# Attention in groups of four heads and channel mix in 384-token units: one change to a fused kernel on one Trainium2 core

## The chip, the core and the metric

The kernel runs on one core of one Trainium2 chip. The metric is the device time of one execution in microseconds (us); every kernel tried was run four times, alternating with the kernel before on the same chip. The engines are TensorE (PE in the profile, PEld for its weight loads), VectorE (DVE), ScalarE (ACT), GpSimd (POOL) and the DMA engines, fed from queues on SyncE (SP), ScalarE and GpSimd. Each of VectorE, ScalarE and GpSimd works through its own instruction list in the order that the compiled program gives it.

## The reference, cut to what matters

```python
# q, k, v: (8 batches, 8 heads, 576 tokens, 64) fp32
q_s = softmax(q, axis=-1)                 # over the 64 channels of a token
k_s = softmax(k, axis=2)                  # over the 576 tokens
kv  = einsum('bhsd,bhse->bhde', k_s, v)   # 64 x 64 per head
x   = einsum('bhsd,bhde->bhse', q_s, kv)  # then heads side by side: (8, 576, 512)

x_prev = x shifted by one token
xk = mu_k * x + (1 - mu_k) * x_prev       # the same with mu_r for xr
k  = relu(xk @ w_k)                       # 512 x 1024
v  = (k * k) @ w_v                        # 1024 x 512
out = sigmoid(xr @ w_r) * v               # w_r 512 x 512
```

## The kernel before

The kernel works batch by batch. Attention handles two heads at a time (a "pair", 4 per batch): the two heads lie on the two halves of the partitions, and products have 64 weight columns. v is loaded by GpSimd's queue, which casts fp32 to bf16 on the way, two loads per pair. The parts that the change touches:

```python
def emit_attention_pair(b, hp):
    nc.gpsimd.dma_start(out=va[0:64, :, 0:64],    in_=v_src_A)    # casting loads
    nc.gpsimd.dma_start(out=va[64:128, :, 65:129], in_=v_src_B)
    nc.scalar.activation(out=eqk, in_=QKt[:, hp, :, :], func=ACT.Exp)
    # ... VectorE: sum, reciprocal, qs = eq / sum
    for j in range(J):                                            # J = 9
        nc.tensor.matmul(kvp[:], lhsT=eqk[:, 1, j, :], rhs=va[:, j, :], ...)   # 64 columns
    # ... two ScalarE copies scale kv into kvpad; 9 transposes; two copies into qtpad
    nc.tensor.matmul(otp[0:64, 0:512],   lhsT=kvApad, rhs=qTApad[:, 0:512], ...)
    # ... three more: head A and B, columns 0:512 and 512:576
    nc.scalar.copy(out=xb[:, 64:64 + S], in_=otp[:])
    # ... VectorE: four scalings by mu or 1-mu, three additions (the last 64 tokens apart)

for b in range(B):                        # channel mix of batch b, attention of b + 1
    for fc in range(FT):                  # 8 steps: first matmuls, 288 tokens at a time
        emit_t3(b, fc); maybe_pairs(slot)   # the 4 pairs fall in these 8 steps
    for m in range(4):                    # 4 steps: output matmuls, 128 tokens at a time
        emit_t45(b, m)
    # ... 64 tokens per batch are left over and handled for two batches together
```

The softmax here doesn't subtract the row's maximum and nothing guards it: scores larger than these inputs give would overflow.

## Time and profile before

| what | value |
|---|---|
| time, median | 279.24 us at first, 279.57 with one more run |
| TensorE busy | 228.8 us, 83% |
| VectorE busy | 194.7 us, 70% |
| a steady batch | 28.4 us, and 2.6 us more in every second one |

These lines of the page of the profile before are the busy time by engine, the span in 40 slices (a digit is the busy share in tenths; PEclk is TensorE's granted clock), GpSimd's DMA queue, and the chain of waits by engine and by line.

```profile
PE 228.8 (83%) x1648; PEld 133.5 (48%) x1648; DVE 194.7 (70%) x636; ACT 154.4 (56%) x357; POOL 50.3 (18%) x73
PE   0045423999999899979997999989989999999992
DVE  5199804999689935997499828994899659755421
DMA  7999999993599447992599258944663352033044
q0 software_dynamic: 39984, 7.34, 36.6%
PE 56%; DVE 21%; DMA 12%; ACT 6%; issue 2%; POOL 1%
```

TensorE is nearly full from the eighth slice on (48 us), while VectorE swings between 9 and 3. The casting loads (of v, and once of the weights) make 39,984 packets and take 36.6% of the DMA engines' time for 7.3 MB.

TensorE stops at 36.6 us and starts again at 45.5, when a load of v that was queued behind the weights lands.

The windows view of before gives busy time per engine in the two halves of one steady batch: first matmuls with attention, then output matmuls. In both kernels its columns are start and end, length, then busy us (and instructions) of PE, PEld, DVE, ACT, POOL, then clock, DMA share and GB/s. (The DMA share counts the whole time of every packet that starts in the stretch, so it can exceed 1.)

```profile
105.70:123.20 17.50, 15.75 (x149) 10.61 (x147) 15.44 (x56) 15.17 (x37) 5.99 (x8) 1.00 1.22 195
123.20:134.10 10.90, 10.90 (x54) 4.89 (x54) 7.46 (x21) 3.50 (x9) 0.00 (x0) 1.00 0.44 57
```

In the first half TensorE and VectorE are both near 90%, each waiting for the other; in the second TensorE is full and VectorE, even with what it carried over, is not.

Durations overlap on VectorE, so costs are best read from start to start. Three lines of the timeline show it: each scaling is listed with 0.36 us, but the next starts 0.28 us later.

```profile
119.86 0.36 DVE L218 TENSOR_SCALAR xmk<-xb_111,muk 128x576 bf16<-128x576 bf16 x1
120.14 0.36 DVE L228 TENSOR_SCALAR xmr<-xb_111,mur 128x576 bf16<-128x576 bf16 x1
120.42 0.36 DVE L222 TENSOR_SCALAR xpk<-xb_111,omk 128x576 bf16<-128x576 bf16 x1
```

### The profile page before, as it was taken

The page shows a single profiled execution, that of the slowest core. Times are in us where ns is not written, and L with a number is a line of the kernel's source. Part 1 is how long each engine was busy: PE and PEld are TensorE (multiplying, and loading weights), DVE is VectorE, ACT ScalarE, POOL GpSimd, SP SyncE. Part 2 cuts the span into 40 slices and gives each one's busy share as a digit, 9 for nine tenths or more (in the row PEclk, how much of TensorE's full clock was granted, in tenths as well). Part 3 has the DMA queues.
Part 4 walks back from the last instruction along what each step waited for, and adds up shares of the span by engine and source line. Part 5 has one row for each costly group of instructions (what it writes and reads, how often), then busy time and mean ns, then how long its engine had stood idle before and what let it go on. Part 6 is the DMA issues. An engine that isn't in the chain of part 4 may idle for free.

```text
span 277.1 us, 4740 instructions
## 1 busy us (share of the span) xinstructions
PE 228.8 (83%) x1648; PEld 133.5 (48%) x1648; DVE 194.7 (70%) x636; ACT 154.4 (56%) x357; POOL 50.3 (18%) x73
## 2 busy tenths in 40 slices
PE   0045423999999899979997999989989999999992
PEld 0034302664466345644564446634654456546540
DVE  5199804999689935997499828994899659755421
ACT  2438403696398626892689239862887167626420
POOL 6027202230033102330224004210322020000000
PEclk9998555699999999999999999999999999999998
DMA  7999999993599447992599258944663352033044
GB/s 248 221 277 241 260 230 77 310 97 21 114 207 234 26 100 113 241 168 43 106 236 194 42 112 198 243 28 97 80 43 24 76 107 31 2 75 77 0 106 85
DMA packets 55368, 35.97 MB, mean 130 GB/s; under 512 B 40496, under 2 KB 42032, under 8 KB 55344
## 3 DMA queue, kind: packets, MB, share of 16 engines
q0 software_dynamic: 39984, 7.34, 36.6%
q1 hardware_dynamic: 10560, 18.88, 27.4%
q10 hardware_dynamic: 4800, 9.44, 11.4%
q8 instruction: 13, 0.21, 0.3%
q14 instruction: 11, 0.09, 0.1%
HBM read 33.56 MB, written 9.44 MB: 155 GB/s over the span
## 4 chain that ended last, share of the span: by engine, by line
PE 56%; DVE 21%; DMA 12%; ACT 6%; issue 2%; POOL 1%
PE vp L275 20%; PE kfpt L252 12%; PE rp L280 10%; DMA vaug_108<-in_v_dram 8%; PE kvp L179 3%; DMA mur<-in_moe_mu_r_dram 3%; PE vpt L299 2%; PE otp L205 2%; PE qtp L194 2%; DVE xk_b L225 2%; DVE xmr L228 2%; DVE rsum L169 2%; DVE qs L173 2%; DVE xr_b L235 2%; DVE xpr L232 2%
## 5 line engine op out<-in xcount | busy, mean ns | idle before, releaser
L252 PE MATMUL kfpt<-xk_b,wk_bf 128*128 128x288 bf16 x512 | 77.9, 293 | 4.2 <-DMA wk_bf<-in_moe_w_k_dram 3.6
L252 PEld LDWEIGHTS <-wk_bf 128*128 128x128 bf16 x512 | 46.1, 99 | 25.9 <-issue 6.4
L256 ACT ACTIVATE rel<-kfpt 128x288 bf16<-128x288 f32 x128 | 48.0, 408 | 8.0 <-PE kfpt L252 6.1
L284 ACT ACTIVATE th<-rp 128x512 f32<-128x512 f32 x32 | 19.1, 597 | 57.5 <-PE rp L280 57.4
L287 DVE SCALAR_TENSOR_TENSOR ot<-th,vp 128x512 f32<-128x512 f32 x32 | 22.0, 687 | 36.0 <-ACT th L284 36.0
L194 PE MATMUL qtp<-ident,qs 128*64 128x128 bf16 x288 | 25.3, 235 | 25.2 <-DVE qs L173 17.0
L163 ACT ACTIVATE eqk<-QKt 128x1152 bf16<-128x1152 f32 x32 | 37.2, 1168 | 1.7 <-PE kvp L179 1.4
L280 PE MATMUL rp<-wr_bf,xr_b 128*128 128x512 bf16 x128 | 33.4, 379 | 0.0
L194 PEld LDWEIGHTS <-qs 128*64 128x64 bf16 x288 | 20.2, 120 | 22.7 <-DVE qs L173 17.0
L179 PEld LDWEIGHTS <-eqk 128*64 128x64 bf16 x288 | 20.1, 119 | 19.3 <-issue 17.7
L169 DVE TENSOR_REDUCE rsum<-eqk 128x9 f32<-128x576 bf16 x32 | 23.3, 730 | 4.2 <-ACT eqk L163 4.2
L173 DVE TENSOR_TENSOR qs<-eqk,rrec 128x576 bf16<-128x576 bf16 x32 | 24.0, 753 | 0.6
L280 PEld LDWEIGHTS <-xr_b 128*128 128x128 bf16 x128 | 12.5, 98 | 15.3 <-issue 0.5
L159 POOL DMA_DIRECT2D vaug_108<-in_v_dram x11 | 8.0, 732 | 60.2 <-PE kvp L179 57.8
L159 POOL DMA_DIRECT2D vaug_104<-in_v_dram x11 | 8.3, 759 | 54.3 <-PE kvp L179 50.6
L214 ACT CAST xb_103<-otp 128x576 bf16<-128x576 f32 x11 | 7.0, 638 | 19.2 <-PE otp L211 19.2
L179 PE MATMUL kvp<-vaug_108,eqk 128*64 128x130 bf16 x99 | 9.6, 240 | 8.9 <-DMA vaug_108<-in_v_dram 8.9
L159 POOL DMA_DIRECT2D vaug_112<-in_v_dram x10 | 7.7, 769 | 46.0 <-PE kvp L179 46.0
L225 DVE TENSOR_TENSOR xk_b<-xmk,xpk 128x576 bf16<-128x576 bf16 x32 | 14.3, 447 | 0.0
L235 DVE TENSOR_TENSOR xr_b<-xmr,xpr 128x512 bf16<-128x512 bf16 x32 | 13.3, 415 | 0.0
L199 ACT COPY qtpad_105<-qtp 64x576 bf16<-64x576 bf16 x11 | 6.9, 628 | 8.4 <-PE qtp L194 8.4
L179 PE MATMUL kvp<-vaug_104,eqk 128*64 128x130 bf16 x99 | 9.9, 240 | 0.0
(227 smaller groups left out, 387.8 us busy)
## 6 DMA issues: line engine op xcount, KB each, us to landing
out_dram<-ot SPq DMA_DIRECT2D x64, 128.0 KB, 2.4
QKt<-in_q_dram SPq DMA_DIRECT2D x7, 1152.0 KB, 8.4
QKt<-in_k_dram ACTq DMA_DIRECT2D x7, 1152.0 KB, 10.5
vaug_104<-in_v_dram POOLq DMA_DIRECT2D x22, 72.0 KB, 6.2
vaug_108<-in_v_dram POOLq DMA_DIRECT2D x22, 72.0 KB, 6.3
vaug_112<-in_v_dram POOLq DMA_DIRECT2D x20, 72.0 KB, 6.4
QKt<-in_q_dram SPq DMA_DIRECT2D x4, 288.0 KB, 5.5
QKt<-in_k_dram ACTq DMA_DIRECT2D x4, 288.0 KB, 5.8
```

The costliest lines, as they stand in the source:

```text
L159: nc.gpsimd.dma_start(out=va[0:64, :, 0:64], in_=v_src_A)
L163: nc.scalar.activation(out=eqk[:].rearrange("p a j d -> p (a j d)"), in_=QKt[:, hp, :, :].rearrange("p a f -> p (a f)"), func=ACT.Exp)
L169: nc.vector.reduce_sum(out=rsum[:], in_=eq, axis=AX.X)
L173: nc.vector.tensor_tensor(out=qs[:], in0=eq, in1=rrec[:, :, None].to_broadcast((128, J, D)), op=ALU.mult)
L179: nc.tensor.matmul(kvp[:], lhsT=eqk[:, 1, j, :], rhs=va[:, j, :], start=(j == 0), stop=(j == J - 1))
L194: nc.tensor.transpose(out=qtp[:, 128 * j:128 * j + 128], in_=qs[:, j, :], identity=ident[:])
L225: nc.vector.tensor_tensor(out=xk_b[:, hp, :], in0=xmk[:], in1=xpk[:], op=ALU.add)
L252: nc.tensor.matmul(kfp, lhsT=wk_bf[:, ct, fc * 128:(fc + 1) * 128], rhs=xk_b[:, ct, c0:c1], start=(ct == 0), stop=(ct == CT - 1))
L256: nc.scalar.activation(out=rel[:, 0:(c1 - c0)], in_=kfp, func=ACT.Relu)
L275: nc.tensor.matmul(vp[0:M, 0:C], lhsT=k2[:, ft, t0:t0 + M], rhs=wv_bf[:, ft, :], start=(ft == 0), stop=(ft == FT - 1))
L280: nc.tensor.matmul(rp[0:M, 0:C], lhsT=xr_b[:, ct, t0:t0 + M], rhs=wr_bf[:, ct, :], start=(ct == 0), stop=(ct == CT - 1))
L287: nc.vector.scalar_tensor_tensor(out=ot[0:M, :], in0=th[0:M, :], scalar=1.0, in1=vp[0:M, 0:C], op0=ALU.add, op1=ALU.mult)
```

## The change

Its intent: make attention's matmuls use the whole array, make fewer and larger instructions everywhere, load v by plain fp32 loads, and spread attention evenly over the channel mix. Four heads form a group (2 per batch). The four 64x64 kv matrices of a group become two 128x128 block-diagonal weights w. The channel mix runs in units of 384 tokens over pairs of batches (1152 tokens, 3 units), so no 64-token rest remains. A unit has 14 steps (8 of first matmuls, 6 of output matmuls), and attention's steps are handed out over all of them.

```diff
-        nc.gpsimd.dma_start(out=va[0:64, :, 0:64], in_=v_src_A)
-        nc.gpsimd.dma_start(out=va[64:128, :, 65:129], in_=v_src_B)
+        for i, src in enumerate((q, k, v)):            # plain fp32, 4 heads each
+            nc.sync.dma_start(out=t[:, i, :, :], in_=ap)
+        nc.gpsimd.tensor_copy(out=vv[:, :, 0:128]..., in_=t[:, 2, :, :]...)   # cast
 ...
-            nc.tensor.matmul(kvp[:], lhsT=eqk[:, 1, j, :], rhs=va[:, j, :], ...)
+            for hf in range(2):
+                r = slice(64 * hf, 64 * hf + 64)
+                nc.tensor.matmul(kvp[:, hf, 0:129], lhsT=eqk[r, 1, j, :, :]..., rhs=vv[r, j, 0:129], ...)
+        for hf in range(2):                            # block-diagonal by a mask
+            nc.vector.scalar_tensor_tensor(out=w[:, hf, :], in0=kvp[:, hf, 0:128],
+                                           scalar=rz[:, hf:hf + 1], in1=mask[:], ...)
 ...
-        nc.tensor.matmul(otp[0:64, 0:512], lhsT=kvApad, rhs=qTApad[:, 0:512], ...)   # and 3 more
+                nc.tensor.matmul(xp[:, a, 0:288], lhsT=w[:, hf, :], rhs=qt[:, hf, 288 * a:288 * a + 288], ...)
 ...
-        for (c0, c1) in [(0, 288), (288, S)]:
+    def unit(n):                                       # 384 tokens
+        for fc in range(FT):
+            # 4 matmuls of 384 columns, one Relu, one square; yield
+        for m in range(U // 128):
+            # tanh part; yield; value part and output; yield
 ...
-    nc.gpsimd.dma_start(out=wv_st[:], in_=wv_src)
-    nc.vector.tensor_scalar(out=wv_bf[:], in0=wv_st[:], scalar1=0.5, ...)
+        for h in range(2):                             # after the casts of batch 0
+            nc.gpsimd.dma_start(out=wv_h, in_=ap)
+            nc.vector.tensor_scalar(out=wv_h, in0=wv_h, scalar1=0.5, ...)
 ...
+    for n in range(NU):                                # 12 units
+        goal = min((B - 1) * ASTEPS, ASTEPS + int(ASTEPS * n / 1.5) + 1)
+        for i, _ in enumerate(unit(n)):
+            want = goal0 + (goal - goal0) * (i + 1) // MSTEPS
+            # take attention steps until `want`
```

## The prediction

> **What bounds the kernel now.** TensorE, in three unequal stages. (1) Start: the timeline shows TensorE idle from 36.6 us to 45.5 us behind one v load (`vaug_108`), which the chain of waits carries as 21.3 us of DMA: it was queued behind the weights. Until then DMA moves 220 to 280 GB/s. (2) Seven steady batches of 28.4 us, plus 2.6 us for a tail in every second. The back-to-back starts in the timeline give, per batch, about 8.0 us of first matmuls, 10.4 us of output matmuls and 4 x 1.5 us of attention, 24.4 in all; some 4 us are stalls. They fall in the attention half, where VectorE is busy without a gap for 20 us, while in the output half VectorE idles (36.0 us waiting for tanh). (3) Last batch and tails, 27 us, pure TensorE at 0.97 clock.
>
> **What the change does to each engine.**
> - Channel mix on TensorE: same work. 384 matmuls of 384 columns instead of 512 of 288, and 432 of 512 as before. Estimate from starts 125 ns (288 columns) and 216 ns (512): 13 us per unit, 156 us in all.
> - Attention on TensorE: per four heads 18 kv matmuls on 64 rows, 9 transposes, 4 products of 288 columns: estimate 1.7 to 2.2 us at 62 ns a small one, against 3.06 us for two pairs. Saves 14 to 21 us over sixteen groups.
> - VectorE: one 1152-element pass replaces two of 576, two k2 squares of 288+224+64 become one of 384, no tail pieces. Net of overlap (start to start: scale 0.28, add 0.36, reduce 0.66, output 0.60 us) I estimate 7.7 us per group, 0.27 per square, 0.6 per output: about 21.4 us per batch against 22.8. But w moves here from ScalarE.
> - ScalarE: 6.6 us of attention per two pairs falls to 3.6. It was not the limit.
> - GpSimd: 64 casting loads (36.6% of DMA time in tiny packets, the queue table) vanish; 16 casts of v appear. The Trainium skill, "SBUF — State Buffer", section "Who interferes with whom", says that GpSimd and the two-port VectorE instructions lock each other out. The trace of before has no such cast; I allow 1 to 2 us per group.
>
> **Critical path.** Attention is now spread over all steps of a unit, so VectorE's load is even. In an attention unit (1.5 groups): TensorE 13 + 3.3 = 16.3 us, VectorE about 15.7 plus locks; with stalls 17 to 18. About 8.5 such units, then three of 13 us.
>
> **Start.** Batches 0 and 1 (7.1 MB) and weights (5.2 MB) must arrive before attention of batch 1 ends; at 250 to 270 GB/s that is 46 to 49 us, so the start gains little; but more is done by then.
>
> Sum: 49 + 8.5 x 17.5 + 3 x 13 + 3 = 240 us.
>
> **Predicted: 240 us, range 227 to 256** (8 in 10). Chances: faster by over 2% 0.95, within 2% 0.03, slower 0.02.
>
> **What would show it.** Right: TensorE waits for loads until 45 to 50 us; VectorE the busiest or within 10% of TensorE up to about 200 us; three last units of 13 us with TensorE alone; attention matmuls half as long; software DMA packets fall to the weights. Wrong: unit period near 20 us with TensorE waiting for w, qt or k2 (VectorE-bound); VectorE scale instructions stretched beyond 0.36 us beside GpSimd casts; loads arriving late in steady state (about 205 GB/s is needed by my estimate).
>
> **What would make it wrong.** A cast far above 2 us, or VectorE's order delaying w and qt: then 255 or more. The two row halves running at once, and a start over before 40 us: then 225.

## More of the kernel before

The experiments ran on three chips (0, 7 and 5), on which the kernel before had medians of 279.49, 278.34 and 278.53 us; the four runs of the changed kernel were made before them and not repeated, so a difference of about 1 us from it says nothing.

The start is seen in three lines of the timeline of before (start, duration, engine, line, operation, and in brackets the idle time before it and what ended it).

```profile
35.73 0.90 PE L252 MATMUL kfpt<-xk_b,wk_bf 128*128 128x288 bf16 x3
43.30 1.23 DVE L333 TENSOR_SCALAR wv_bf<-wv_st 128x4096 bf16<-128x4096 bf16 x1 [8.68 <-DMA wv_st<-in_moe_w_v_dram]
45.49 0.29 PE L179 MATMUL kvp<-vaug_108,eqk 128*64 128x130 bf16 x1 [8.86 <-DMA vaug_108<-in_v_dram]
```

## The result, and the profile after

The changed kernel took 247.67 us (median of 4 runs, 246.63 to 249.17) against 279.57. The ratio is 0.884, with a 95% interval of 0.878 to 0.891. A ratio here is the mean time of one kernel's fast runs over that of the other's of the same rounds, so it is not quite the ratio of the medians. The profiled run took 246.7 us, of which the profile's span shows 244.5.

The lines of the page of after that answer to those of before:

```profile
PE 190.5 (78%) x1296; PEld 103.2 (42%) x1313; DVE 186.2 (76%) x434; ACT 120.0 (49%) x197; POOL 33.8 (14%) x32
PE   0335200898987969797979999979999999999992
DVE  1489312999999999999999999999969844252521
DMA  6999999921997587898881303203113031322313
q0 software_dynamic: 2208, 2.62, 6.1%
PE 49%; DVE 27%; DMA 14%; ACT 4%; POOL 2%; issue 1%; DVEq 0%; ACTq 0%
```

TensorE lost 38 us of busy time. VectorE has 434 instead of 636 instructions, and its row is now an unbroken run of nines from 43 us to about 177 us. That is the picture of a bound moving: TensorE's row has sevens and eights just there. Two windows of after say it in numbers, the first of 100 us with attention running, the second the last three units:

```profile
60.00:160.00 100.00, 88.60 (x647) 47.94 (x654) 99.37 (x226) 58.14 (x97) 14.90 (x9) 1.00 0.64 196
200.60:239.50 38.90, 38.74 (x202) 19.87 (x203) 14.80 (x33) 17.16 (x33) 0.00 (x0) 1.00 0.27 61
```

VectorE is busy for 99.4 of 100 us and TensorE for 88.6; at the end TensorE is full and VectorE at 38%. TensorE's granted clock dips to 0.5 in part of the start of this profile. The runs show no cost of this dip: the two at a mean clock of 0.95 took 246.6 and 246.7 us, the two at 0.99 took 248.6 and 249.2.

The start looks as before, but its cause is another. These lines are from the timeline of after:

```profile
19.04 1.56 POOL L117 DMA_DIRECT2D wv_bf<-in_moe_w_v_dram  x2
29.16 1.15 PE L168 MATMUL kvp<-vv_108,eqk 64*128 64x129 bf16 x18 [3.36 <-ACT xb_106 L195]
35.54 0.69 DVE L118 TENSOR_SCALAR wv_bf<-wv_bf 128x2048 bf16<-128x2048 bf16 x1 [8.28 <-DMA wv_bf<-in_moe_w_v_dram]
41.09 0.69 DVE L118 TENSOR_SCALAR wv_bf<-wv_bf 128x2048 bf16<-128x2048 bf16 x1 [4.85 <-DMA wv_bf<-in_moe_w_v_dram]
44.00 1.44 PE L222 MATMUL kfp<-xk,wk_bf 128*128 128x384 bf16 x4 [13.68 <-DVE xk L210]
```

TensorE waits 13.7 us for xk, which VectorE makes. VectorE had what it needed for xk (ScalarE had copied the second group's attention out by about 30 us), but next in its list stood the two halvings of the second weight, and they waited for their DMA until 35.5 and 41.1 us. Everything behind them waited too. The weight landed late because GpSimd issued it only at 19 us: in its list the casts of v came first, and each of those waited for its load.

The third thing to see is what GpSimd's cast does to VectorE:

```profile
85.19 0.37 DVE L206 TENSOR_SCALAR xm<-xb_110,mu 128x576 bf16<-128x576 bf16 x1
85.28 1.29 POOL L146 CAST vv_100<-raw 128x1152 bf16<-128x1152 f32 x1 [10.18 <-PE kvp L168]
85.47 1.25 DVE L208 TENSOR_SCALAR xq<-xb_110,om 128x576 bf16<-128x576 bf16 x1
86.65 0.36 DVE L206 TENSOR_SCALAR xm<-xb_110,mu 128x576 bf16<-128x576 bf16 x1
```

The scaling at 85.47 takes 1.25 us instead of 0.36 and ends just after the cast does. The Trainium skill, "SBUF — State Buffer", section "Who interferes with whom", says that GpSimd and VectorE share a port pair as an exclusive lock, and that whichever comes first holds it for its whole instruction while the other is blocked (on VectorE's side, for instructions in a two-port mode or with two inputs in SBUF). The trace agrees: of the 11 casts from 40 us on, nine lengthen one VectorE instruction, by 0.68 to 0.97 us above that line's median, 7.8 us together. Beside the other two, at 133.9 and 143.2 us, VectorE runs at its usual pace, and the second of these casts takes 3.05 us itself.

### The profile page after: what moved, and what is told of

Same layout as the page of the kernel before. It is cut to its first block, busy times and chain, and to the rows that moved or that the text cites. A ratio compares the mean times of both kernels' runs of the same rounds, so it can differ in the third digit from the quotient of the medians.

```text
span 244.5 us, 3656 instructions
## 1 busy us (share of the span) xinstructions
PE 190.5 (78%) x1296; PEld 103.2 (42%) x1313; DVE 186.2 (76%) x434; ACT 120.0 (49%) x197; POOL 33.8 (14%) x32
## 3 DMA queue, kind: packets, MB, share of 16 engines
q0 software_dynamic: 2208, 2.62, 6.1%
## 4 chain that ended last, share of the span: by engine, by line
PE 49%; DVE 27%; DMA 14%; ACT 4%; POOL 2%; issue 1%; DVEq 0%; ACTq 0%
PE vp L239 21%; PE kfp L222 14%; PE rp L232 9%; DMA wv_bf<-in_moe_w_v_dram 9%; DVE qs L160 5%; DVE xq L208 4%; DMA raw<-in_v_dram 4%; DVE xm L206 3%; PE xp L192 2%; DVE xr L210 2%; DVE xk L210 2%; DVE rsum L156 2%; DVE ot L242 2%; ACT eqk L150 2%; PE qtp L182 2%; DMA raw<-in_q_dram 2%
## 5 line engine op out<-in xcount | busy, mean ns | idle before, releaser
L222 PE MATMUL kfp<-xk,wk_bf 128*128 128x384 bf16 x384 | 69.4, 331 | 15.9 <-DVE xk L210 15.1
L226 ACT ACTIVATE rel<-kfp 128x384 bf16<-128x384 f32 x96 | 46.1, 495 | 38.0 <-PE kfp L222 32.5
L150 ACT ACTIVATE eqk<-raw 128x1152 bf16<-128x1152 f32 x32 | 36.7, 1163 | 34.5 <-DMA raw<-in_q_dram 15.1
L232 PE MATMUL rp<-wr_bf,xr 128*128 128x512 bf16 x130 | 36.4, 379 | 0.7
L156 DVE TENSOR_REDUCE rsum<-eqk 128x18 f32<-128x1152 bf16 x16 | 21.5, 1345 | 8.5 <-ACT eqk L150 8.5
L160 DVE TENSOR_TENSOR qs<-eqk,rrec 128x1152 bf16<-128x1152 bf16 x16 | 21.6, 1351 | 0.1
L192 PE MATMUL xp<-qt,w 128*128 128x288 bf16 x64 | 12.1, 295 | 10.2 <-DVE qt L184 6.8
L232 PEld LDWEIGHTS <-xr 128*128 128x128 bf16 x144 | 13.7, 98 | 13.3
L146 POOL CAST vv_100<-raw 128x1152 bf16<-128x1152 f32 x6 | 8.2, 1371 | 49.3 <-PE kvp L168 42.2
L146 POOL CAST vv_108<-raw 128x1152 bf16<-128x1152 f32 x5 | 10.8, 2164 | 27.6 <-PE kvp L168 16.9
L146 POOL CAST vv_104<-raw 128x1152 bf16<-128x1152 f32 x5 | 7.7, 1547 | 44.3 <-DMA raw<-in_v_dram 22.8
L210 DVE TENSOR_TENSOR xr<-xm,xq 128x1152 bf16<-128x1152 bf16 x16 | 12.7, 794 | 0.0
## 6 DMA issues: line engine op xcount, KB each, us to landing
wv_bf<-in_moe_w_v_dram POOLq DMA_DIRECT2D x2, 512.0 KB, 18.9
```

The source lines that it names most:

```text
L146: nc.gpsimd.tensor_copy(out=vv[:, :, 0:128].rearrange("p j (u d) -> p j u d", u=2), in_=t[:, 2, :, :].rearrange("p u (j d) -> p j u d", d=D))
L150: nc.scalar.activation(out=eqk[:, i, :, :, :], in_=t[:, i, :, :].rearrange("p u (j d) -> p j u d", d=D), func=ACT.Exp)
L156: nc.vector.reduce_sum(out=rsum[:], in_=eq, axis=AX.X)
L160: nc.vector.tensor_tensor(out=qs[:].rearrange("p j (u d) -> p (j u) d", u=2), in0=eq, in1=rrec[:, :, None].to_broadcast((128, 2 * J, D)), ...
L192: nc.tensor.matmul(xp[:, a, 0:288], lhsT=w[:, hf, :], rhs=qt[:, hf, 288 * a:288 * a + 288], start=True, stop=True)
L210: nc.vector.tensor_tensor(out=dst[:, 2 * g:2 * g + 2, c0:c0 + S], in0=xm[:], in1=xq[:], op=ALU.add)
```

## The experiments

Theory after reading the traces: (a) VectorE bounds the stage in which attention runs; (b) the lock with GpSimd's casts is part of that; (c) the start is set by VectorE's fixed order behind the halving, not by the loads as such. The main rivals: (a') TensorE, or the chain of latencies, still bounds; (c') the loads set the start. Eleven kernels were run, all correct. Times are medians of four runs; the changed kernel had 247.67.

| kernel | time | against the changed kernel |
|---|---|---|
| halving taken off VectorE | 237.68 | -10.0 |
| cast of v on ScalarE | 233.28 | -14.4 |
| both | 233.16 | -14.5 |
| transposed q copied by ScalarE | 241.89 | -5.8 |
| casting v loads again | 247.10 | -0.6 |
| ... and attention in pairs | 272.38 | +24.7 |
| attention in the first 8 steps only | 252.39 | +4.7 |
| slower pacing | 241.54 | -6.1 |
| no halving, cast split | 230.66 | -17.0 |
| ... and slower pacing | 228.75 | -18.9 |
| ... and q copied by ScalarE | 226.71 | -21.0 |

### The halving taken off VectorE

```diff
-            nc.vector.tensor_scalar(out=wv_h, in0=wv_h, scalar1=0.5, ...)
-            nc.scalar.activation(out=rel[:], in_=kfp[:, 0:U], func=ACT.Relu)
+            nc.scalar.activation(out=rel[:], in_=kfp[:, 0:U], func=ACT.Relu, scale=0.5 ** 0.5)
```

> The halving of the second weight is taken off VectorE (the Relu takes a scale of the root of one half instead; nothing else changes). Theory: between 27 and 41 us VectorE sat idle in its fixed order behind this halving, whose weight landed only at 41 us, while the second group's mix work was ready; TensorE's 13.7 us gap came from that. Expected: the gap at 30 to 44 us shrinks to under 6 us, VectorE's dense stretch starts near 30 us, and the time falls by 6 to 11 us to about 237 to 242. Rival, the prediction's: loads of batch 1 and the weights arriving set the start; then the gap stays until 40 us or later and the gain is under 3 us.

Measured: 237.68 us, 10.0 us less (ratio to before 0.853). The timeline of this kernel at the place of the gap:

```profile
29.27 1.16 PE L166 MATMUL kvp<-vv,eqk 64*128 64x129 bf16 x18 [3.51 <-ACT xb L193]
32.77 1.44 PE L220 MATMUL kfp<-xk,wk_bf 128*128 128x384 bf16 x4 [2.34 <-DVE xk L208]
```

The wait for xk is 2.3 us instead of 13.7, and the first matmuls go on at 32.8 instead of 44.0 us. The loads are the same. So the start was not set by the arrival of the loads; the halving in VectorE's order held it.

### The cast of v on ScalarE

```diff
-        nc.gpsimd.tensor_copy(out=vv[:, :, 0:128]..., in_=t[:, 2, :, :]...)
+        nc.scalar.copy(out=vv[:, :, 0:128]..., in_=t[:, 2, :, :]...)
```

> The cast of v moves from GpSimd to ScalarE. Theory: VectorE bounds the stage from 44 to about 180 us, and each GpSimd cast lengthens one VectorE instruction by about 0.9 us (9 of them, 7.8 us in that stage). Expected: no VectorE scale or square above 0.6 us any more and 5 to 8 us less, about 240 to 243. Rival (VectorE is busy but the order of TensorE and the loads set the pace): under 2 us gained, or a loss, since ScalarE's own queue gets 16 x 1.16 us more.

Measured: 233.28 us, 14.4 us less, twice the expectation: a miss in size. No VectorE scale or square is stretched any more, as expected. The surplus is in the timeline of this kernel's start:

```profile
8.05 0.77 POOL L117 DMA_DIRECT2D wv_bf<-in_moe_w_v_dram  x1 [1.56 <-DMA wk_bf<-in_moe_w_k_dram]
29.48 0.69 DVE L118 TENSOR_SCALAR wv_bf<-wv_bf 128x2048 bf16<-128x2048 bf16 x1
31.41 0.69 DVE L118 TENSOR_SCALAR wv_bf<-wv_bf 128x2048 bf16<-128x2048 bf16 x1
37.66 3.67 PE L222 MATMUL kfp<-xk,wk_bf 128*128 128x384 bf16 x11 [1.68 <-DVE xk L210]
```

With no casts in its list GpSimd issues the second weight at 8 us instead of 19, so the halvings wait for nothing. The first matmuls go on at 37.7 us, 6.3 us earlier than in the changed kernel. From there to the tenth unit this kernel needs 149.4 us (until 187.1), the changed one 156.6 (44.0 to 200.6): 7.2 us less, about the size of the lock. (From the second unit on, with the start quite left out, it is 6.4 us.)

### Both together

> No halving and the cast on ScalarE together. If the two causes are separate (start, and steady stage) the gains add: 11 to 18 us, about 230 to 237. If both only feed the same wait, the sum is less than the larger plus 2 us.

Measured: 233.16 us, within 0.2 us of the ScalarE cast alone. The gains do not add; of the two outcomes the second came true. The ScalarE cast had already removed the halving's wait by another way, so there was nothing left to remove. But it starts 5 us later than the kernel without halving (37.5 against 32.8 us). The weights, asked for earlier, share the DMA engines with the second group's loads: the exponential of that group's q starts at 14.7 us with the cast on ScalarE, at 10.9 us in the changed kernel. That the sharing is the whole of the 5 us is argued, not shown. A rival was not tested: on ScalarE each cast now stands in front of exponentials and waits there for its v, the second until 20.2 us.

### The copy of the transposed q on ScalarE

```diff
-        nc.vector.tensor_copy(out=qt..., in_=qtp...)
+        nc.scalar.copy(out=qt..., in_=qtp...)
```

> The copy of the transposed q out of PSUM (0.75 us on VectorE, about 0.67 net, 13 of them in the VectorE-bound stage) moves to ScalarE, where I expect about 1.15 us. Theory VectorE-bound: 5 to 9 us less, about 239 to 243. Rival (latency of the chain kv, transpose, copy, product bounds): no gain or slower, since that link gets longer.

Measured: 241.89 us, 5.8 us less, inside the range for a VectorE bound; the start gap is unchanged (a single wait of 15.8 us). A chain of latencies would have grown longer. This supports (a).

### Casting v loads again

```diff
-        for i, src in enumerate((q, k, v)):
+        for i, src in enumerate((q, k)):
+        for u in range(2):
+            nc.gpsimd.dma_start(out=vv[:, :, 64 * u:64 * u + 64], in_=ap)   # four vv buffers
-        nc.gpsimd.tensor_copy(out=vv[:, :, 0:128]..., in_=t[:, 2, :, :]...)
```

> One part undone: v comes again by casting loads on the GpSimd queue (two per group, straight into the bf16 tile; four v buffers so that nothing is overwritten), with no cast on any engine; all else is the changed kernel. If the gain came from the loads becoming plain ones (fewer, larger packets), this gives back much: 255 or more. My theory: in the steady stage loads are not the limit, so what counts is the lock between GpSimd's cast and VectorE, which this takes away too: 238 to 246, with software packets up by some 37000 and VectorE free of stretched instructions.

Measured: 247.10 us, no difference to the changed kernel (247.67). Software packets are back at 39,584. Two effects nearly cancel. Without the casts the steady stage is shorter: from the first matmuls after the second batch's kv (53.7 us) to the tenth unit (201.1 us) it takes 147.4 us, where the changed kernel takes 156.6. But the start is later by 9.7 us (53.7 against 44.0): the first v lands only after TensorE has waited 23.1 us for it. (Six more first matmuls, 1 us, are done by then, so each of the two differences is some 8 to 9 us.) The halving has a part in this start too: GpSimd, with the loads of v in its list, issues the second weight only at 31 us, and VectorE waits for it again, as the first two of these lines show.

```profile
44.78 0.69 DVE L126 TENSOR_SCALAR wv_bf<-wv_bf 128x2048 bf16<-128x2048 bf16 x1 [6.08 <-DMA wv_bf<-in_moe_w_v_dram]
47.13 1.44 PE L228 MATMUL kfp<-xk,wk_bf 128*128 128x384 bf16 x4 [10.65 <-DVE xk L216]
48.89 0.99 POOL L73 DMA_DIRECT2D vv<-in_v_dram  x1 [2.58 <-DMA wv_bf<-in_moe_w_v_dram]
49.24 0.75 DVE L212 TENSOR_SCALAR xm<-xb,mu 128x576 bf16<-128x576 bf16 x1
```

One expectation was missed: VectorE is not free of stretched instructions. Nine scalings still took 0.57 to 0.82 us instead of 0.36, each while GpSimd issued a load, as in the last two lines. So in this kernel, with the halving in VectorE's list, the plain loads were not a gain in themselves; they bought an earlier start and paid for it with GpSimd's lock. Casting loads without the halving were not run.

### Attention in pairs again

```diff
+    def attention(b, g):
+        for u in range(2):
+            yield from pair(b, g, u, t)      # the old attention: 64 weight columns,
+    def pair(b, g, u, t): ...                # two heads, kvpad and qtpad, old channel order
-        ... tag="mm", bufs=4
+        ... tag="mm", bufs=3                 # three instead of four
```

> The headline undone alone: attention again two heads at a time with the old 64-column products, old copies and old channel order, inside the new 384-token units, new pacing, and the same casting v loads as the previous kernel (its control; three instead of four PSUM tiles for the units[...]). VectorE's work per four heads is by my count equal (7.5 us against 7.7 net), TensorE's 3.1 us against 2.0, ScalarE's 6.6 against 3.6. Theory VectorE-bound: within 6 us of the control. Rival, TensorE-bound: the 14 attention groups of the steady stage cost 14 to 20 us more than the control.

Measured: 272.38 us, 25.3 us more than its control above, and a ratio to before of 0.975 (0.969 to 0.980, too near to 2% for a verdict: "unclear"). The VectorE theory's "within 6 us" fell, and even the rival's 14 to 20 was too little. The windows line of this kernel:

```profile
60.00:160.00 100.00, 99.70 (x700) 50.15 (x699) 89.68 (x244) 73.09 (x155) 24.68 (x34) 1.00 0.92 161
```

Its chain of waits by engine, from its page:

```profile
PE 79%; DMA 16%; DVE 2%; ACT 1%; issue 1%; POOL 0%; DVEq 0%; POOLq 0%
```

Two more things differ from the control: three PSUM tiles instead of four, and four smaller loads of v per group instead of two. Neither holds TensorE back here, since it idles for only 0.3 us of these 100.

Now TensorE is the full one (99.7) and VectorE has slack (89.7): with pairs TensorE bounds, with groups of four VectorE. The theory was right about the changed kernel and wrong about how near the other bound was: it took the pairs' TensorE cost from the estimate of 1.5 us per pair. The timeline of TensorE in this kernel shows more:

```profile
110.96 1.47 PE L231 MATMUL kfp<-xk,wk_bf 128*128 128x384 bf16 x8
112.36 0.60 PE L208 MATMUL otp<-qt,w 128*64 128x512 bf16 x4
112.89 0.82 PE L231 MATMUL kfp<-xk,wk_bf 128*128 128x384 bf16 x4
113.65 0.71 PE L186 MATMUL kvp<-vv,eqk 128*64 128x130 bf16 x9
114.29 0.82 PE L231 MATMUL kfp<-xk,wk_bf 128*128 128x384 bf16 x4
115.05 0.69 PE L197 MATMUL qtp<-ident,qs 128*64 128x128 bf16 x9
115.67 1.47 PE L231 MATMUL kfp<-xk,wk_bf 128*128 128x384 bf16 x8
```

From start to start the products take 0.53 us, the kv matmuls 0.64, the transposes 0.62: 1.79 us per pair. And each unit piece in front of them takes longer than its matmuls: 8 first matmuls last 1.40 us from start to start, where the changed kernel's TensorE timeline has 1.30 in front of its products:

```profile
101.36 1.46 PE L222 MATMUL kfp<-xk,wk_bf 128*128 128x384 bf16 x8
102.66 0.41 PE L192 MATMUL xp<-qt,w 128*128 128x288 bf16 x2
```

The Trainium skill, "TensorEngine Tiling (Array Packing)", section "Key Properties", says that changing the tiling mode drains TensorE. The weights' sizes in these lines (128*64 against 128*128) are taken here as the mode, and the trace agrees with about 0.1 us per change into the 64-column mode. The way back costs as much (the next first matmul starts 0.15 us after the last kv matmul, where two kv matmuls start 0.06 us apart), but that is in the 1.79 already. Three changes per pair make a pair 2.1 us, two pairs 4.2; with the changes in and out taken off, two pairs come to about 3.0, the 3.06 of the prediction. In the group of four the transposes and products stay in the units' mode and pay nothing; only its kv matmuls, on 64 rows, change it. I had counted 3.06 against 2.0. The trace of before had the cost too: there a kv matmul starts 0.22 us after a first matmul of 288 columns, where two first matmuls start 0.12 us apart.

### Attention in the first 8 steps only

```diff
-                want = goal0 + (goal - goal0) * (i + 1) // MSTEPS
+                want = goal0 + (goal - goal0) * min(i + 1, FT) // FT
```

> The even spread undone alone: the attention steps of a unit are handed out over its first 8 steps (the first matmuls) instead of all 14, as in the old kernel. Theory of the prediction (the gain of the steady stage comes from VectorE's load being even): VectorE idles again in the output half, TensorE waits for qs, qt and k2 in the first half: 8 us or more slower than the changed kernel, 255 to 262. Rival (the queues and the scheduler even it out anyway): under 3 us.

Measured: 252.39 us, 4.7 us more: between the two expectations. The even spread is worth something, but a good part of the unevenness is taken up anyway: from 60 to 160 us VectorE stays 98.8 us busy here, as its queue carries work over into the output steps.

### Slower pacing

```diff
-            goal = min((B - 1) * ASTEPS, ASTEPS + int(ASTEPS * n / 1.5) + 1)
+            goal = min((B - 1) * ASTEPS, ASTEPS + int(14 * n / 1.5) + 1)
```

> Only the pacing slower: attention is handed out at 14 instead of 16 steps per batch of units, so it ends about one unit later (still ahead of every unit that reads it). Theory: while attention runs VectorE bounds, afterwards TensorE alone with VectorE half idle (3.3 units of 13 us); a unit moved into the first stage costs VectorE 4 us instead of TensorE 13: 4 to 9 us less, 239 to 244. Rival (TensorE or latency bounds all along): no change.

Measured: 241.54 us, 6.1 us less, as expected for (a). The work is the same; only a unit's worth of TensorE time now runs while VectorE is the bound instead of after it.

### No halving, and the cast split by batch

```diff
+        # no halving, as above, and:
+        (nc.gpsimd.tensor_copy if b == 0 else nc.scalar.copy)(out=vv[:, :, 0:128]..., ...)
```

> No halving, and the cast of v on GpSimd for the first batch but on ScalarE from the second batch on. It separates what the ScalarE cast did (14 us, twice my expectation) into two parts. Theory: about 7 us were the lock in the steady stage, the other 6 to 7 were the start, because with no cast in front of them GpSimd issued the second weight at 8 us instead of 19 us, so the halving no longer blocked VectorE. Then this kernel starts as the one without halving does (first matmuls again at about 33 us) and runs the steady stage as the ScalarE cast does (150 us): 229 to 232. Rival (the ScalarE cast has only one effect, on the start): no better than 236.

Measured: 230.66 us, 7.0 us less than the kernel without halving (237.68), whose start it keeps (first matmuls again at 31.4 us). The two medians come from two chips. In the profiles the tenth unit starts 5.9 us earlier (185.1 against 191.0 us), and 0.7 us of that is there when the second unit starts (53.5 against 54.2), so the lock of the steady stage by itself is 5.2 us here, against the 7.8 read from the stretched instructions. About half of the ScalarE cast's 14.4 us was the start.

### The version that beats both

> The same with the slower pacing (14 instead of 16), a version meant to beat both kernels. If VectorE still bounds while attention runs, 4 to 6 us less than the previous one: 224 to 228. If the freed VectorE has made TensorE the bound already, under 2 us.

Measured: 228.75 us, 1.9 us less, under the expected 4 to 6: the second outcome.

> The same with the copy of the transposed q on ScalarE too. VectorE loses another 9 us of work, but TensorE needs 188 us for the arithmetic by my count and starts in earnest at 33 us. If VectorE still bounds: 4 to 6 us less again, 219 to 223. If TensorE or ScalarE (now some 155 us busy) takes over: within 2 us of the previous one, or slower.

Measured: 226.71 us, 2.0 us less (ratio to before 0.814), on the border of the second outcome. The windows lines of these two kernels, in this order, explain the shrinking returns:

```profile
60.00:160.00 100.00, 97.04 (x686) 52.07 (x686) 98.24 (x236) 71.60 (x114) 0.00 (x0) 1.00 0.60 188
```

```profile
60.00:160.00 100.00, 98.19 (x699) 52.69 (x698) 92.35 (x226) 76.81 (x122) 0.00 (x0) 1.00 0.60 188
```

TensorE has risen from 88.6 to 98.2 of 100 us and VectorE fallen from 99.4 to 92.4. The bound has moved back to TensorE. What remains is mostly the start, where TensorE's first long stretch begins only near 30 us.

## Why the prediction was right or wrong

The measured 247.67 us lies in the range of 227 to 256, and the direction was right; the point, 240, was 7.7 us low.

- **What bounds before.** TensorE, in three stages. Right; the pairs experiment shows that even in the new frame TensorE is the full engine as long as attention is in pairs.
- **Attention on TensorE, "1.7 to 2.2 us" per group.** Right: 18 kv matmuls in 0.63 us, 9 transposes in 0.68, 4 products in 0.65 by the chain of waits, 1.96 in all. From start to start, as the pairs are counted, it is 0.63, 0.50 and 0.49, with the change of mode 1.7. **"Against 3.06 us for two pairs"** was mis-sized: about 4.2 in the pairs experiment, and its control is faster by 25.3 us, not by "14 to 21". The missing term is the drain at the change of tiling mode, some 0.09 us in and 0.09 us out, six times in two pairs.
- **VectorE, "7.7 us per group".** Right. From start to start after: reduce 1.26, reciprocal 0.18, qs 1.27, q copy 0.67, w 0.5 with its reciprocal 0.1, shift 0.1, eight scalings at 0.28, two additions at 0.67, 7.7 in sum.
- **The lock, "1 to 2 us per group".** The mechanism was there, at about 0.9 us per cast that met a VectorE instruction; the time it cost was 5 to 7 us (5.2 by the split cast, 7.2 by the ScalarE cast), at most half of the 14 us or more that this allows for 14 groups.
- **A unit with attention, "17 to 18 us".** Right: from 44.0 to 200.6 us are nine units less 8 of the 32 first matmuls of the first, 8.9 units of 17.6 us. The prediction had 8.5 of them. Some of what it named as signs against it came true as well: TensorE waited for qs, qt and w, but the unit period stayed at 17.6 us and not near 20; scalings were stretched to 1.25 us; and the two row halves ran at once (18 kv matmuls in 0.63 us, where the pairs need 0.64 for 9). The 225 us named with the row halves did not come, since VectorE was the bound and the start was not over before 40 us.
- **The start, "batches 0 and 1 and weights must arrive ... 46 to 49 us".** This step failed, and its number was near (44.0) by luck. The loads as such did not set it. With the halving gone and the loads unchanged the first matmuls went on at 32.8 us. DMA also moved more than the 250 to 270 GB/s assumed (293 to 394 GB/s in the seven slices after the first). The compiled order of instructions, which could be read before the run, had the halvings in VectorE's list ahead of the second group's mixing; I did not ask what an instruction that waits for a DMA does to those behind it.
- **The sum.** Start 5 us too long; attention stage 156.6 instead of 148.8; last units right (38.9); the end after them 5.0 instead of 3; and the time is 2.2 us above the span, which I had left out. Together about 7 us, of the 7.7.
- **The loads.** "Software DMA packets fall to the weights" came true (2,208), but the casting loads cost the changed kernel nothing when put back (247.10).

So where did 32 us come from? The four-head attention alone accounts for 25 us (pairs against control), and spreading the steps over the whole unit is worth about 5 us. The plain loads gave nothing net. The 384-token units were not undone alone; all that the pairs kernel keeps of the change, these units and the even spread among it, gave 6.0 us (272.38 against 278.34 on that chip). These are single undoings of parts that interact, so they need not add up exactly.

## What to carry to other kernels

An instruction that waits for a DMA blocks everything behind it on its engine (here that held TensorE for 13.7 us), so look, for each late load, at which engine's list holds its first user, and move that work to where its wait harms nothing, or fold it into an instruction that is there anyway. When a change takes much from the bounding engine, ask at once which engine is next: here VectorE at 99%, and folding one halving away, moving a copy and the casts to ScalarE, and a slower pacing were together worth another 21 us. Small matmuls in another tiling mode cost more than their columns: here about 0.1 us for each change of mode, in and out.

## What the Trainium skill lacked or had wrong

- "TensorEngine Tiling (Array Packing)", "Key Properties", says that a change of tiling mode drains TensorE, but gives no cost. Here 8 matmuls in front of a change to 64 columns took 1.40 us instead of 1.30, about 0.1 us per change, and the way back costs as much. With three changes in and out in each of 32 pairs (an estimate of some 18 us of TensorE's time) this was a part of the 25.3 us that the pairs cost.
- "SBUF — State Buffer", "Who interferes with whom", states the lock as measured here (VectorE instructions of 0.36 us took 1.25 beside a cast) and that the other side is blocked as well. The runs add a size for this pair of instructions: a cast of 1152 fp32 elements per partition on GpSimd took 1.15 us undisturbed and up to 3.74 us when VectorE was busy, and cost VectorE about 0.9 us where it met one of its instructions, 5 to 7 us of the whole.
- "PSUM — Partial Sum Buffer", "Engine vs sequencer instructions", has the queues of ScalarE, VectorE and GpSimd in strict order, but no page gives the cost that an instruction waiting for a DMA puts on independent work behind it: 13.7 us of TensorE's time, 10.0 us of the whole, in this kernel.
